# Attention values loaded in longer runs, into a third buffer, in another order

## The chip, the cores and the metric

One core of one Trainium2 chip runs the whole program. The metric is the device time of one execution in microseconds (us). A measurement of this kernel can tell about 0.2% (1.7 us) from no change.

## The reference

Three layers follow each other. The first is chunked local attention: each chunk of 32 queries sees 8 memory keys, 16 keys to the left, its own 32 and 8 to the right.

```python
def _attn_ref(q, k, v, mem_k, mem_v):          # B, H, S, D = 2, 8, 768, 64
    for c in range(S // 32):
        l_start, r_end = max(0, 32 * c - 16), min(S, 32 * c + 32 + 8)
        k_full = np.concatenate([mem_k, k[:, :, l_start:r_end]], axis=2)
        v_full = np.concatenate([mem_v, v[:, :, l_start:r_end]], axis=2)
        scores = scale * np.matmul(q[:, :, 32 * c:32 * c + 32], k_full.transpose(0, 1, 3, 2))
        a = np.exp(scores - np.max(scores, axis=-1, keepdims=True))
        a = a / (np.sum(a, axis=-1, keepdims=True) + 1e-09)
        out[:, :, 32 * c:32 * c + 32] = np.matmul(a, v_full)
...
def _moe_ref(x, domain_probs, w1, w2):         # 1536 tokens, 512 wide, 4 experts, 1024 inner
    p = domain_probs / (domain_probs.sum(-1, keepdims=True) + 1e-09)
    for e in range(E):
        out += p[:, e:e + 1] * (np.maximum(x @ w1[e], 0.0) @ w2[e])
...
def _moe2_ref(x, w_in, w_out, alpha):          # 2048 inner
    h = x @ w_in
    return (np.maximum(h, 0.0) + alpha * np.minimum(h, 0.0)) @ w_out
```

All data are float32.

## The kernel before

**Work.** Attention is cut into 24 half-units (`half_unit`). One is a block of 128 queries, that is four windows of 32, of four heads. The half-units of a block's eight heads follow each other, and so do those of the two batches. The two later layers run over the tokens in tiles, `gemm1` and `gemm2`, with each float32 number cut into a high and a low part, so that TensorE does three products for one.

**One half-unit.** TensorE makes the scores (32 small matmuls into `two`, which has one buffer). VectorE takes the row maximum `mx` and subtracts it into `pe_ring`; ScalarE makes the exponential in place. TensorE transposes (`t`), ScalarE copies that to `pt_ring`. TensorE multiplies with the values (16 matmuls into `x`); the values carry a column of ones, so that `x` also holds the sum of the weights. VectorE adds 1e-9 (`dn`), takes the reciprocal (`rd`) and scales into `xs_ring`. TensorE transposes once more (`xt`), and ScalarE copies that to `acc`, the input of the next layer. `prep_x` splits `acc` into `xh` and `xl`.

**Values.** A tile `v` has 128 rows, two heads of 64 keys each. For each pair of heads and each window a row holds 130 numbers: 65 for the upper head and 65 for the lower one, and of these two one half is zero, so that one matmul over 128 rows gives both heads. The zeros are written once, by memsets on GpSimd and VectorE, and the loads fill the rest. The array in memory has 520 numbers (2080 bytes) in a row for one half-unit; in the tile they are laid out in 8 pieces of 65 numbers (260 bytes) with a gap of 65 after each. There are `RINGV` buffers of values (2) and `RING` of queries and keys (4).

**Order.** Every engine runs its instructions in the order in which the program writes them; nothing is moved afterwards. The generators and their due times in `now` set that order while the program is written. `load_half(hu + RING)` stands behind the score matmuls of half-unit `hu`, and `load_v(hu + RINGV)` behind its `x` matmuls, both in SyncE's queue. Each DMA uses one of eight semaphores in turn, so that an issue can also have to wait for the DMA that used its semaphore before.

**Two stretches.** Up to 57.65 us, 16 cycles (`att_cycle`) do attention alone: a cycle takes the scores of half-unit `m`, the `xt` of `m-3`, the `x` of `m-2`, then `keep_warm` (4 or 5 matmuls on zeros, whose result nobody reads) and the `t` of `m-1`. From 57.65 to 91.7 us the other half-units are put between the matmuls of the first tile of the second layer (`att_poll`). After that TensorE has the two matrix layers alone.

Of the kernel before, what the change touches and what calls it, by code (L numbers as in the profile page):

```python
# [10 lines left out]
F32 = mybir.dt.float32  # L11
# [7 lines left out]
B, H, S, D = 2, 8, 768, 64  # L19
CH, LEFT, RIGHT, MEM = 32, 16, 8, 8  # L20
BLK = 128
WIN = CH
NW = BLK // WIN
# [8 lines left out]
P = 128  # L32
KD = DM // P
HH = H // 2
HP = HH // 2
QW, KW, VW = HP * BLK, HP * SPAN, HP * (D + 1)
# [29 lines left out]
def tile_kernel(ctx: ExitStack, tc: tile.TileContext, qk, v, wa, wq, dpt, alpha, out):  # L66
    nc = tc.nc
    scale = 1.0 / float(D) ** 0.5
    pe_, dve, act, pool, sync = (Pinned(tc, e) for e in (nc.tensor, nc.vector, nc.scalar, nc.gpsimd, nc.sync))
# [3 lines left out]
    bp = ctx.enter_context(tc.tile_pool(name="bp", bufs=1))  # L73
# [7 lines left out]
    def bank(name):  # L81
        taken[0] += 1
        if more and taken[0] % 4 == 0:
            return more[0].tile([P, 512], F32, tag="pm", name=name)
        return ps.tile([P, 512], F32, tag="ps", name=name)
# [67 lines left out]
    def prep_x(c0, n, fast):  # L153
        cs = slice(c0, c0 + n)
        b11, b12 = acc[:, 0:2, 0, cs], acc[:, 0:2, 1, cs]
        b21, b22 = acc[:, 2:4, 0, cs], acc[:, 2:4, 1, cs]

        st = bp.tile([P, 3, 2, n], F32, tag="fr" if change[0] and c0 // n % 2 else "st", name=f"st{c0}")
        e = dve if fast else pool
        sub = ALU.subtract  # L160
        act.copy(xh[:, 0:4, cs], acc[:, :, 0, cs])
        e.tensor_tensor(out=st[:, 0], in0=b12, in1=b11, op=sub)
        yield
        e.tensor_tensor(out=st[:, 1], in0=b22, in1=st[:, 0], op=sub)
        act.copy(xh[:, 4:6, cs], b22)
        yield
        e.tensor_tensor(out=st[:, 2], in0=b22, in1=b12, op=sub)
        pool.tensor_tensor(out=xl[:, 0:4, cs], in0=acc[:, :, 0, cs], in1=xh[:, 0:4, cs].bitcast(F32), op=sub)
        yield
        for z in (0, 1):  # L170
            r = slice(6 + 4 * z, 10 + 4 * z)
            t_ = st[:, z:z + 2].rearrange("p a b n -> p (a b) n")
            if z == 1:
                e.tensor_tensor(out=st[:, 1], in0=b21, in1=st[:, 1], op=sub)
                yield
            act.copy(xh[:, r, cs], t_)
            if z == 0:
                pool.tensor_tensor(out=xl[:, 4:6, cs], in0=b22, in1=xh[:, 4:6, cs].bitcast(F32), op=sub)
            yield
            e.tensor_tensor(out=xl[:, r, cs], in0=t_, in1=xh[:, r, cs].bitcast(F32), op=sub)  # L180
            yield
# [6 lines left out]
    def mm(*a, n, took=None, **kw):  # L188
        pe_.matmul(*a, **kw)
        now[0] += took or 0.013 + n / 2.4e3  # L190


    qk_t = [bp.tile([P, QW + KW], F32, tag="ggB", bufs=4, name=f"qk{i}") for i in range(RING)]
    v_t = [bp.tile([P, HP, NW, 2, D + 1], F32, tag="w2", bufs=4, name=f"v{i}") for i in range(RINGV)]
    for vt in v_t:
        for e in range(2):
            (pool, dve)[e].memset(vt[(1 - e) * D:(2 - e) * D, :, :, e], 0.0)
    pe_ring = bp.tile([P, 2, HP, 2, KEYS], F32, tag="ft", bufs=3, name="pe_ring")
    pt_ring = bp.tile([P, 2, HP, BLK], F32, tag="fr", name="pt_ring")
    xs_ring = bp.tile([P, 2, HP, 2, D], F32, tag="ft", bufs=3, name="xs_ring")  # L200

    def load_half(hu):
        if hu >= 2 * NU:
            return
        sync.dma_start(qk_t[hu % RING], qk[hu // 2, :, hu % 2])

    def load_v(hu):
        if hu >= 2 * NU:
            return
        for e in range(2):  # L210
            rows = slice(e * D, (e + 1) * D)
            sync.dma_start(v_t[hu % RINGV][rows, :, :, e].rearrange("p z w d -> p (z w) d"),
                           v[hu // 2, rows, hu % 2].rearrange("p (a d) -> p a d", d=D + 1))

    def half_unit(u, half):

        hu = 2 * u + half
        qv = qk_t[hu % RING][:, :QW].rearrange("p (z q) -> p z q", q=BLK)
        kv = qk_t[hu % RING][:, QW:].rearrange("p (z k) -> p z k", k=SPAN)
        vv = v_t[hu % RINGV].rearrange("p z w e d -> p z w (e d)")  # L220
        c, ab = divmod(u, 2)
        cols = slice(c * BLK, (c + 1) * BLK)
        hs = slice(2 * half, 2 * half + 2)
        nm = f"{u}_{half}"

        win = [slice(w * WIN, (w + 1) * WIN) for w in range(NW)]
        s_ps = two[:, :, :HP * KEYS].rearrange("p e (z k) -> p e z k", k=KEYS)
        now[0] += T_SW
        for z in range(HP):
            for w in range(NW):  # L230
                for e in range(2):
                    rows = slice(e * D, (e + 1) * D)
                    mm(s_ps[win[w], e, z], qv[rows, z, win[w]], kv[rows, z, w * STEP:w * STEP + KEYS], n=KEYS,
                       took=T_S, start=True, stop=True)
        load_half(hu + RING)
        mx = cp.tile([P, 2, HP], F32, tag="mx", bufs=4, name=f"mx{nm}")
        dve.tensor_reduce(out=mx, in_=s_ps, axis=AX.X, op=ALU.max)
        pe = pe_ring[:, hu % 2]
        dve.tensor_tensor(
            out=pe.rearrange("p z e k -> p e z k"), in0=s_ps,  # L240
            in1=mx.unsqueeze(3).to_broadcast([P, 2, HP, KEYS]), op=ALU.subtract,
        )
        yield LATE
        act.activation(pe, pe, AF.Exp, scale=scale)
        yield LAT[0]
        t_ps = bank(f"t{nm}")[:, :HP * BLK].rearrange("p (z q) -> p z q", q=BLK)
        now[0] += T_SW
        for z in range(HP):
            pe_.transpose(t_ps[:, z], pe[:, z].rearrange("p e k -> p (e k)"), ident)
            now[0] += T_T  # L250
        pt = pt_ring[:, hu % 2]
        act.copy(pt, t_ps)
        yield LAT[1]
        x_ps = bank(f"x{nm}")[:, :2 * VW].rearrange("p (z e d) -> p z e d", e=2, d=D + 1)
        now[0] += T_SW
        for z in range(HP):
            for w in range(NW):
                mm(x_ps[win[w], z].rearrange("p e d -> p (e d)"), pt[:, z, win[w]], vv[:, z, w], n=2 * (D + 1),
                   took=T_X, start=True, stop=True)
        load_v(hu + RINGV)  # L260
        dn = cp.tile([P, HP, 2, 1], F32, tag="dn", bufs=2, name=f"dn{nm}")
        dve.tensor_scalar_add(dn, x_ps[:, :, :, D:D + 1], 1e-9)
        rd = cp.tile([P, HP, 2, 1], F32, tag="rd", bufs=2, name=f"rd{nm}")
        dve.reciprocal(rd, dn)
        xs = xs_ring[:, hu % 2]
        dve.tensor_tensor(out=xs, in0=x_ps[:, :, :, :D], in1=rd.to_broadcast([P, HP, 2, D]), op=ALU.mult)
        yield LAT[2]
        xt_ps = bank(f"xt{nm}")[:, :2 * BLK].rearrange("p (c q) -> p c q", q=BLK)
        now[0] += T_SW
        for z in range(HP):  # L270
            pe_.transpose(xt_ps[:, z], xs[:, z].rearrange("p e d -> p (e d)"), ident)
            now[0] += T_T
        act.copy(acc[:, hs, ab, cols], xt_ps)
        if ab == 1 and half == 1:
            while att["x"] < c:
                yield 0.2
            for _ in prep_x(c * BLK, BLK, c in FAST):
                yield X_STEP[c]
            att["x"] = c + 1
# [47 lines left out]
    def att_cycle():  # L327
# [14 lines left out]
        def at(hu, stage):  # L342
            if hu in live and att["stage"][hu] == stage:
                advance(live[hu])

        x = live[m] = [now[0], half_unit(*divmod(m, 2)), m]
        att["live"].append(x)
        att["next"] += 1
# [15 lines left out]
    raws, w1, w2 = {}, {}, {}  # L364
# [68 lines left out]
    def weights():  # L433
        for p in range(NP):
            yield from prep_w(p)
# [49 lines left out]
    def stream(name, gen):  # L485
        streams[name] = [0.0, None, gen]
# [213 lines left out]
        order += [(1, k), (2, k - 1)]  # L700
    order += [(2, len(tiles) - 1)]

    for i in range(2):
        load_half(i)
        load_v(i)
    load_half(2)
    stream("w", weights())
    streams["w"][0] = PREP0
    acts = {}
# [7 lines left out]
    for i, (what, k) in enumerate(order):  # L717
        p, c0, n = tiles[k]
# [41 lines left out]
T_S, T_X, T_T, T_SW = 0.017, 0.06, 0.11, 0.1  # L760
# [11 lines left out]
T_CONV = 18.0  # L772
DT_X = 0.35
RING = 4
RINGV = 2
WARM = 18


# [72 lines left out]
```

## Time and profile before

| what | value |
|---|---|
| median of 3 runs | 858.92 us (858.74 to 859.26) |
| the profiled execution, its own time | 859.42 us |
| its span, first to last instruction | 857.6 us |
| TensorE busy | 827.4 us, 96% of the span |
| VectorE, ScalarE, GpSimd busy | 593.8, 337.7, 575.3 us |
| mean granted TensorE clock | 0.984 |
| queue of the loads and stores | 50752 packets, 70.75 MB |

The time of the execution is 1.8 us more than its span. Share of busy time is a mean over stages with different limits; the rows below separate them. Kilobytes of a transfer are of 1024 bytes, GB/s are of 10^9.

### The profile page before, as it was taken

To read this page: it belongs to the slowest core of one execution; us is meant where nothing else is said; L and a number is where in the kernel's file an instruction comes from. 1 tells how busy PE (TensorE), PEld (TensorE's weight loads), DVE (VectorE), ACT (ScalarE), POOL (GpSimd) and SP (SyncE) were. 2 spreads that over 40 slices of the span, in tenths; PEclk is the share of its full clock that TensorE was granted. 3 is DMA by queue.
4 is the path that set the end of the run, shared out by engine and by line. 5 is a ranking of instruction groups with operands and counts; after the bars stand their busy time and mean duration, and the time that the engine had idled before them with its cause. 6 is when DMAs were issued, how large, how long until landed. Compare 5 with 4: busy or idle time off the path is not lost.

```text
span 857.6 us, 15042 instructions
## 1 busy us (share of the span) xinstructions
PE 827.4 (96%) x5659; PEld 801.5 (93%) x5659; DVE 593.8 (69%) x1159; ACT 337.7 (39%) x754; POOL 575.3 (67%) x606
## 2 busy tenths in 40 slices
PE   7878999999999999999999999998899999999998
PEld 5655899999999999999999999997799999999998
DVE  3665847767677676777766786779777766776655
ACT  2544643223222231332332332325465645645442
POOL 2527566778659777678776777748576787764831
PEclk9998999999999999999999999999799999999999
DMA  9897202133213223213222212101012222111103
GB/s 217 185 214 174 63 24 73 56 100 105 87 38 102 89 80 100 87 38 120 89 80 82 86 63 88 72 1 50 25 50 74 75 87 98 63 62 38 62 1 148
DMA packets 50825, 71.71 MB, mean 84 GB/s; under 512 B 29120, under 2 KB 33344, under 8 KB 50752
## 3 DMA queue, kind: packets, MB, share of 16 engines
q1 hardware_dynamic: 50752, 70.75, 27.9%
q8 instruction: 44, 0.72, 0.4%
q14 instruction: 29, 0.24, 0.1%
HBM read 59.18 MB, written 11.56 MB: 82 GB/s over the span
## 4 chain that ended last, share of the span: by engine, by line
PE 85%; DMA 5%; DVE 4%; issue 2%; ACT 1%; SPq 1%; POOL 1%; POOLq 0%; DVEq 0%; ACTq 0%
PE y L60 45%; PE c L60 11%; PE a L60 11%; PE d L60 11%; PE b L60 5%; DMA v<-in_v 4%; DVE st L60 2%; PE x L60 1%; SPq L60 1%; DVE xl L60 1%; PE keep L60 1%; DMA qk<-in_qk 1%; ACT xh L60 1%; POOL gg L60 1%; DVE acc L60 1%
## 5 line engine op out<-in xcount | busy, mean ns | idle before, releaser
L60 PE MATMUL y<-gg,wh 128*128 128x384 f32 x1540 | 407.3, 341 | 7.1 <-POOL gg L60 4.4
L60 PEld LDWEIGHTS y<-gg,wh 128*128 128x128 f32 x1540 | 282.0, 190 | 11.0 <-POOL gg L60 6.8
L60 POOL TENSOR_TENSOR gg<-g,gg 128x384 fp32r<-128x384 f32 x192 | 199.6, 1049 | 109.2 <-ACT gg L60 98.9
L60 PE MATMUL y<-gg,wl 128*128 128x384 f32 (+1 forms) x770 | 260.6, 338 | 0.0
L60 DVE TENSOR_TENSOR acc<-y,acc 128x384 f32<-128x384 f32 x353 | 189.0, 551 | 68.3 <-PE y L60 66.8
L60 ACT CAST gg<-g 128x384 fp32r<-128x384 f32 x192 | 97.9, 512 | 163.7 <-DVE g L60 163.1
L60 POOL TENSOR_TENSOR wl<-raw,wh 128x256 fp32r<-128x256 f32 (+1 forms) x115 | 115.8, 1016 | 54.9 <-PE b L60 33.9
L60 PEld LDWEIGHTS y<-gg,wl 128*128 128x128 f32 x770 | 146.3, 190 | 0.0
L60 ACT COPY u<-a 128x384 f32<-128x384 f32 x48 | 23.1, 481 | 214.1 <-PE a L60 214.1
L60 POOL TENSOR_TENSOR wl<-s,wh 128x256 fp32r<-128x256 f32 x92 | 70.5, 773 | 10.5 <-ACT wh L60 10.3
L60 DVE TENSOR_TENSOR u<-b,u 128x384 f32<-128x384 f32 x48 | 26.7, 557 | 58.4 <-PE b L60 53.6
L60 PE MATMUL c<-xh,wh 128*128 128x384 f32 x192 | 64.7, 337 | 1.7 <-DVE b L60 1.7
L60 PE MATMUL c<-xh,wl 128*128 128x384 f32 x192 | 65.1, 339 | 0.0
L60 PE MATMUL d<-xh,wh 128*128 128x384 f32 x192 | 64.5, 336 | 0.4 <-DVE t L60 0.4
L60 PE MATMUL a<-xh,wh 128*128 128x384 f32 x192 | 64.7, 337 | 0.0
L60 PE MATMUL d<-xl,wh 128*128 128x384 f32 x192 | 64.1, 334 | 0.4 <-issue 0.4
L60 PE MATMUL a<-xl,wh 128*128 128x384 f32 x192 | 64.5, 336 | 0.0
L60 PE MATMUL c<-xl,wh 128*128 128x384 f32 x192 | 64.4, 335 | 0.0
L60 PE MATMUL a<-xh,wl 128*128 128x384 f32 x192 | 64.3, 335 | 0.0
L60 PE MATMUL d<-xh,wl 128*128 128x384 f32 x192 | 64.2, 334 | 0.0
L60 POOL TENSOR_TENSOR fl<-fl,fm 128x512 f32<-128x512 f32 x32 | 41.4, 1295 | 28.4 <-issue 16.8
L60 ACT CAST wh<-raw 128x256 fp32r<-128x256 f32 (+1 forms) x120 | 55.9, 489 | 0.6 <-PE a L60 0.6
(97 smaller groups left out, 1363.5 us busy)
## 6 DMA issues: line engine op xcount, KB each, us to landing
raw<-in_wa SPq DMA_DIRECT2D x32, 512.0 KB, 3.7
fr<-in_wq SPq DMA_DIRECT2D x32, 512.0 KB, 3.9
w2s<-fl SPq DMA_DIRECT2D x32, 256.0 KB, 2.3
raw<-w2s SPq DMA_DIRECT2D x16, 512.0 KB, 3.7
qk<-in_qk SPq DMA_DIRECT2D x24, 312.0 KB, 5.1
v<-in_v SPq DMA_DIRECT2D x48, 130.0 KB, 4.6
pb<-p_dram SPq DMA_DIRECT2D x8, 384.0 KB, 4.1
outT<-acc SPq DMA_DIRECT2D x15, 192.0 KB, 1.9
```

What stands on the lines that cost most here:

```text
L60: return self.tc.keep_in_program_order(f(*a, **kw))
```

## The change

Three things change. A value tile gets the head half as its outermost dimension inside a row, so that the 520 numbers of a load lie in one run of 2080 bytes and not in 8 of 260; an `x` matmul then reads its 130 numbers as two runs of 65, 2080 bytes apart. A third buffer of values is added; it consists of two tiles of one pair of heads each, whose loads are four of 1040-byte runs in place of two. Room for it comes from putting `pt_ring` and `xs_ring` in one tile, `late`. Last, the loads at the start are issued in another order.

```diff
-    v_t = [bp.tile([P, HP, NW, 2, D + 1], F32, tag="w2", bufs=4, name=f"v{i}") for i in range(RINGV)]
+    v_whole = [bp.tile([P, 2, HP, NW, D + 1], F32, tag="w2", bufs=4, name=f"v{i}") for i in range(2)]
+    v_t = [[t[:, :, z] for z in range(HP)] for t in v_whole]
+    v_t += [[bp.tile([P, 2, NW, D + 1], F32, tag="ft", bufs=3, name=f"v2_{z}") for z in range(HP)]]
     for vt in v_t:
-        for e in range(2):
-            (pool, dve)[e].memset(vt[(1 - e) * D:(2 - e) * D, :, :, e], 0.0)
+        for z in range(HP):
+            for e in range(2):
+                (pool, dve)[e].memset(vt[z][(1 - e) * D:(2 - e) * D, e], 0.0)
     pe_ring = bp.tile([P, 2, HP, 2, KEYS], F32, tag="ft", bufs=3, name="pe_ring")
-    pt_ring = bp.tile([P, 2, HP, BLK], F32, tag="fr", name="pt_ring")
-    xs_ring = bp.tile([P, 2, HP, 2, D], F32, tag="ft", bufs=3, name="xs_ring")
+    late = bp.tile([P, 4, HP * BLK], F32, tag="fr", name="late")
+    pt_ring = late[:, 0:2].rearrange("p r (z q) -> p r z q", q=BLK)
+    xs_ring = late[:, 2:4].rearrange("p r (z e d) -> p r z e d", e=2, d=D)
...
+        i = hu % RINGV
         for e in range(2):
             rows = slice(e * D, (e + 1) * D)
-            sync.dma_start(v_t[hu % RINGV][rows, :, :, e].rearrange("p z w d -> p (z w) d"),
-                           v[hu // 2, rows, hu % 2].rearrange("p (a d) -> p a d", d=D + 1))
+            src = v[hu // 2, rows, hu % 2]
+            if i < 2:
+                sync.dma_start(v_whole[i][rows, e].rearrange("p z w d -> p (z w d)"), src)
+            else:
+                for z in range(HP):
+                    sync.dma_start(v_t[i][z][rows, e].rearrange("p w d -> p (w d)"), src[:, z * VW // HP * NW:(z + 1) * VW // HP * NW])
...
-                mm(x_ps[win[w], z].rearrange("p e d -> p (e d)"), pt[:, z, win[w]], vv[:, z, w], n=2 * (D + 1),
-                   took=T_X, start=True, stop=True)
+                mm(x_ps[win[w], z], pt[:, z, win[w]], vv[z][:, :, w], n=2 * (D + 1), took=T_X, start=True, stop=True)
...
+    load_half(0)
     for i in range(2):
-        load_half(i)
+        load_half(i + 1)
         load_v(i)
-    load_half(2)
+    load_v(2)
...
-RINGV = 2
+RINGV = 3
```

On SyncE, at the start of the program, this is the difference; `qk_109` to `qk_112` are the four buffers of queries and keys, `v_113` and `v_114` the two whole buffers of values, `v_0_115` and `v_1_116` the two tiles of the third.

```order
 L60 DMA qk_109<-in_qk 128x624
-L60 DMA v_113<-in_v 64x8x65 x2
 L60 DMA qk_110<-in_qk 128x624
-L60 DMA v_114<-in_v 64x8x65 x2
+L60 DMA v_113<-in_v 64x520 x2
 L60 DMA qk_111<-in_qk 128x624
+L60 DMA v_114<-in_v 64x520 x2
+L60 DMA v_0_115<-in_v 64x260
+L60 DMA v_1_116<-in_v 64x260
+L60 DMA v_0_115<-in_v 64x260
+L60 DMA v_1_116<-in_v 64x260
 L60 DMA qk_109<-in_qk 128x624
```

The second and third loads of queries and keys move ahead of the values that stood before them, and four loads of the third buffer now stand ahead of the fourth and fifth loads of queries and keys.

The next rows are SyncE's queue of the changed program from the same place on, with the semaphores for which each issue waits; `DMAHW0` to `DMAHW7` are those of the DMAs, and a wait for one of them is a wait until an earlier DMA has landed. `raw_0_171` holds the first weights.

```order
L60 DMA v_0_115<-in_v 64x260
L60 DMA v_1_116<-in_v 64x260 [waits DMAHW0_49]
L60 DMA v_0_115<-in_v 64x260 [waits DMAHW1_49]
L60 DMA v_1_116<-in_v 64x260 [waits DMAHW2_49]
L60 DMA qk_109<-in_qk 128x624 [waits DMAHW3_49,PE_49]
L60 DMA qk_112<-in_qk 128x624 [waits DMAHW4_49]
L60 DMA raw_0_171<-in_wa 128x1024 [waits DMAHW5_49]
```

From the ninth DMA on every issue waits for the DMA eight places ahead of it. Before, the fourth and fifth loads of queries and keys were the eighth and ninth DMA of the program; now they are the eleventh and twelfth.

On TensorE, where the third half-unit's values are used for the first time:

```order
-L60 MATMUL xt_1_312<-ident,xs_ring 128x128 x2
-L60 MATMUL x_0_316<-v_113,pt_ring 32x130 x8
-L60 MATMUL keep_333<-xh 128x384 x4
-L60 MATMUL t_1_338<-ident,pe_ring 128x128 x2
+L60 MATMUL xt_1_325<-ident,late 128x128 x2
+L60 MATMUL x_0_329<-v_0_115,late 32x130 x4
+L60 MATMUL x_0_329<-v_1_116,late 32x130 x4
+L60 MATMUL keep_348<-xh 128x384 x4
+L60 MATMUL t_1_353<-ident,pe_ring 128x128 x2
```

Nothing changes its place on TensorE; the `x` matmuls of every third half-unit read two tiles in place of one.

## Rows read from the trace of the kernel before

**Rows 1.** The chain that ended last, its shares by line (page).

```profile
PE y L60 45%; PE c L60 11%; PE a L60 11%; PE d L60 11%; PE b L60 5%; DMA v<-in_v 4%; DVE st L60 2%; PE x L60 1%; SPq L60 1%; DVE xl L60 1%; PE keep L60 1%; DMA qk<-in_qk 1%; ACT xh L60 1%; POOL gg L60 1%; DVE acc L60 1%
```

**Rows 2.** Windows: length, busy time of each engine, TensorE's granted clock, DMA share, GB/s.

```profile
0.00:21.00 21.00, 15.78 (x262) 11.47 (x262) 7.49 (x23) 5.33 (x12) 5.88 (x13) 0.93 0.95 217
21.00:57.65 36.65, 28.91 (x615) 20.96 (x615) 22.22 (x68) 18.09 (x48) 15.58 (x17) 0.95 0.96 198
57.65:76.20 18.55, 13.91 (x293) 9.87 (x292) 11.06 (x34) 10.15 (x27) 11.24 (x12) 0.99 0.96 214
76.20:91.70 15.50, 15.19 (x222) 10.58 (x222) 12.10 (x30) 8.33 (x23) 9.92 (x11) 0.79 0.42 92
...
110.00:550.00 440.00, 440.00 (x2527) 439.93 (x2526) 312.61 (x586) 133.98 (x297) 324.70 (x342) 1.00 0.24 80
```

**Rows 3.** TensorE's waits up to 112 us: us in total, times, longest.

```profile
PE x L60 <- DMA v<-in_v: 10.9, 9, 2.8
PE two L60 <- DMA qk<-in_qk: 2.4, 2, 1.6
PE x L60 <- ACT acc L60: 1.2, 2, 0.9
...
PE x L60 <- ACT xh L60: 0.9, 2, 0.6
PE xt L60 <- DVE xs_ring L60: 0.8, 2, 0.6
```

**Rows 4.** Timeline of TensorE: start, length, operation, count [idle before, releaser].

```profile
44.55 0.98 PE L60 MATMUL keep<-xh 128*128 128x384 f32 x4
...
48.50 1.08 PE L60 MATMUL x<-v,pt_ring 128*32 128x130 f32 x16 [1.99 <-DMA v<-in_v]
49.50 1.65 PE L60 MATMUL keep<-xh 128*128 128x384 f32 x4
```

**Rows 5.** The chain in order of time: start, length, what.

```profile
21.91 0.58 PE x L60 x16
...
24.35 0.58 PE x L60 x16
...
44.67 0.60 SPq L60
...
45.33 7.73 DMA v<-in_v
...
53.15 0.65 PE x L60 x16
```

**Rows 6.** Tile view of the values: issue times (min/median/max ns), time to landing.

```profile
L60 SPq DMA_DIRECT2D v<-in_v x48: 595/596/1385, 1.2 to 85.7; - x48
...
DMA to landing us min/median/max: 3.2/4.6/7.7
```

**Rows 7.** The same view of the queries and keys.

```profile
L60 SPq DMA_DIRECT2D qk<-in_qk x24: 328/379/1655, 0.7 to 70.6; - x24
...
DMA to landing us min/median/max: 3.0/5.1/7.6
```

**Rows 8.** Packets of the whole span (page).

```profile
DMA packets 50825, 71.71 MB, mean 84 GB/s; under 512 B 29120, under 2 KB 33344, under 8 KB 50752
```

**Rows 9.** Two short windows, columns as in group 2.

```profile
10.00:12.00 2.00, 1.66 (x51) 1.36 (x52) 0.99 (x4) 0.14 (x1) 0.00 (x0) 1.00 1.03 417
...
16.00:18.00 2.00, 0.23 (x6) 0.07 (x5) 0.74 (x2) 0.79 (x2) 0.03 (x1) 0.96 1.22 202
```

**Rows 10.** Timeline of TensorE, the second group of score matmuls.

```profile
7.76 0.46 PE L60 MATMUL two<-qk 64*32 64x64 f32 x32 [1.63 <-DMA qk<-in_qk]
```

**Rows 11.** SyncE's queue waiting for earlier DMAs, first 100 us.

```profile
SPq L60 <- DMA v<-in_v: 3.3, 3, 1.9
```

**Rows 12.** The value tiles: the matmuls that read them, the memsets (ns).

```profile
L60 PE MATMUL x<-v,pt_ring x384: 271/274/428, 10.8 to 90.7; 128*32 128x130 f32 x192
...
L60 POOL MEMSET v<- x2: 532/532/532, 2.7 to 3.1; 64x520 f32 x2
```

More of the change, by code (lines that the diff above doesn't have):

```diff
@@ L219, in half_unit @@
         kv = qk_t[hu % RING][:, QW:].rearrange("p (z k) -> p z k", k=SPAN)
-        vv = v_t[hu % RINGV].rearrange("p z w e d -> p z w (e d)")
+        vv = v_t[hu % RINGV]
         c, ab = divmod(u, 2)
```

## The prediction

> **What bounds the kernel now.** The chain that ended last comes first: it shows which engine's work the end hangs on. Four fifths are TensorE's matrix products (`y`, `a`, `b`, `c`, `d`); the one other share above 2% is the wait for value loads, `DMA v<-in_v`, 4% or some 36 us [rows 1]. The windows say where. From 110 to 550 us TensorE is busy for 440.00 of 440 us at the full clock, so whatever is won before that moves everything after it forward one for one. Before 91.7 us TensorE idles: 5.2, 7.7, 4.6 and 0.3 us in the four stretches, and its granted clock is below 1, 0.79 in the last [rows 2]. TensorE's waits name the idle time up to 112 us: 10.9 us for values, 2.4 for queries and keys, and 2.9 for ScalarE and VectorE (1.2, 0.9 and 0.8) [rows 3].
>
> A wait costs a second time. [...] Windows price this: length times missing clock is 21.00 x 0.07, 36.65 x 0.05, 18.55 x 0.01 and 15.50 x 0.21; each times the busy share of its stretch (0.75, 0.79, 0.75, 0.98) makes 1.1 + 1.5 + 0.1 + 3.2 = 5.9 us [rows 2].
>
> Why values are late: with two buffers, the load for half-unit m+2 is issued after the `x` matmuls of m and must be there two cycles later. An undisturbed cycle goes from `x` at 21.91 to `x` at 24.35, 2.44 us. On the chain the load's first issue is at 44.67 us, the second load flies from 45.33 for 7.73 us, and the `x` for it starts at 53.15 [rows 5]. The median landing is 4.6 us, and two issues of 0.6 us stand ahead [rows 6], against 4.9 us for two cycles.
>
> **The change part by part.** *Runs of 2080 bytes.* Of the 29120 packets under 512 bytes, 48 x 64 x 8 = 24576 are value rows of 260 bytes [rows 6, 8]. How much DMA time these take: up to 91.7 us the DMA share times length is 20.0 + 35.2 + 17.8 + 6.5 = 79.5 us, and GB/s times length 17.2 MB. From 110 to 550 us, with long runs, a share of 0.24 moves 80 GB/s, 333 GB/s for a full share [rows 2]. Values are 48 x 133120 bytes = 6.4 MB; the other 10.8 MB at 333 GB/s take 32.5 us, so values take 47 us, at 136 GB/s. In a window of almost only values the queue moved 202 GB/s at a share of 1.22, and 417 GB/s at 1.03 where long runs were on their way [rows 9]; so 333 is no overstatement. In long runs the values take 6.4 / 0.333 = 19 us. The 79.5 us become 52 us. That is the queue's relief, not the program's: the program gets back what TensorE waited.
>
> *The third buffer.* The lead grows to three cycles, 7.3 us. Less about 1.4 us of issues, 5.9 us are left against a landing of 4.6 us in the median (7.7 at most) while the queue is full [rows 6]. With the queue relieved I take landings near the smallest of today, 3.2 us: both parts together should take away nearly all of the 10.9 us. Bounds: all 10.9, or half if the queue stays full. Its price: issues. A third half-unit has four loads in place of two. A load of queries and keys with 128 rows took 0.38 us to issue, a value load with 512 runs 0.6 [rows 6, 7]; with 64 runs I take 0.35 each, so 0.7 us for two and 1.4 for four, no more per cycle than the 1.2 us of today on average. Memsets: half as much again, 0.5 us more on GpSimd [rows 12], long before the first `x`, and VectorE's likewise; nothing.
>
> [...] A load of 130 KB lands in 4.6 us in the median, and one of 312 KB in 5.1 [rows 6, 7]: size hardly matters, and many loads overlap, since three landings, 14.3 us, fit in one cycle. [...] The four pieces are of 65 KB. If they ran one after the other at 3.2 us each, a set would take 12.8 us, 5.5 more than the lead, and eight sets would cost some 44 us; by the rows above they overlap, and cost nothing.
>
> *Order of the first loads.* The second scores waited 1.63 us [rows 10], and 2.4 us went to queries and keys in all [rows 3]. These loads now stand right behind the first, so I take 2.4 us as won. Against it, the fourth load of queries and keys is now the twelfth DMA and waits until the fifth has landed; it should land near 10.5 to 11 us, just when its cycle begins. Bounds: 2.4 us won, or 1 us lost again there.
>
> *`x` in two runs.* The tile's matmuls, 271 to 274 ns of which most is pipelined [rows 12], move on at 0.58 us for 16 [rows 5]. No row shows this read pattern; I take nothing, and as the other bound a doubling, 24 x 0.58 = 14 us. *`late`.* The same instructions wait for the same engines, so nothing.
>
> *What comes next.* Without the waits for values, ScalarE and VectorE have less time between `x` groups. VectorE is busy for 23.2 us of the 34.05 between 57.65 and 91.7 [rows 2], and that stretch shrinks to some 27. I let the 2.9 us that TensorE waits for these engines double. And the queue stays well filled: by 45 us it must bring 20 loads of queries and keys, 17 of values and 1.4 MB of weights and gates, 12.3 MB in 42 us, 293 GB/s of 333. I keep an eighth of the value waits, 1.3 us.
>
> **Sum.** Won: 10.9 + 2.4 + 5.9 = 19.2 us. Given back: 2.9 + 1.3 = 4.2. Net 15.0. The profiled execution took 859.42 us, 0.5 over the median of the runs; 858.92 - 15.0 = 843.9, so 844.
>
> **The rivals.**
> - *The queue stays the bound.* Queries and keys have long runs already and land no sooner than values [rows 6, 7], and 293 of 333 GB/s is close. Half of the value waits (5.5 us) and half of the lost clock (2.9) stay: 19.2 - 2.9 - 8.4 = 7.9 won, 851 us. Against it: 417 GB/s [rows 9].
> - *VectorE becomes the bound of the second stretch.* If it can be no busier than the 12.10 of 15.50 us of its last part [rows 2], its 23.2 us need 29.7 and not 27: 2.5 us less won, 846.5.
> - *Slower: eight DMAs in flight.* Every issue waits for the DMA eight places back. Three half-units take 11 DMAs where they took 9, so a landing time L forces 11/8 x L/3 = 0.46 L per half-unit. Today's mean is (91.7 - 4.6)/24 = 3.63 us, so it decides from a mean L of 7.9 us; at 8.5, 3.9 us each, 24 x 0.27 = 6.5 us, 865. For it: SyncE waited 3.3 us for earlier value loads already [rows 11]. Against it: today's longest landing is 7.7 [rows 6], and the packets get fewer.
> - *The four pieces serialize:* 844 + 44 = 888 us.
> - *`x` doubles:* 844 + 14 = 858 us, no change.
> - *The runs are not joined, and only the third buffer counts:* the loads still need their 79.5 us, and only the last stretch's and the first loads' waits go: some 5 us won, 854.
>
> **Chances.** Forecast 0.70 (its own range 839.5 to 848), queue 0.12, VectorE 0.09, eight in flight 0.03, serialized 0.02, `x` 0.02, not joined 0.02. The range reaches down to 838.5, where all 19.2 us and a little of the engines' waits are won, and up to 851.5 past the queue case. Faster by over 0.2% (1.7 us, about what a measurement of this kernel tells from no change): forecast, queue, VectorE and not joined, 0.93; within it 0.02; slower 0.05.
>
> **What would show it.** Right: TensorE's wait for values below 1.5 us and that for queries and keys near 0 up to 95 us; a granted clock of 0.99 or more up to there; some 20000 packets fewer under 512 bytes; landings of values near 3.2 us; the cycles of the first stretch near 2.5 us, its end near 46 us in place of 57.65; the long busy stretch of TensorE unchanged, only earlier. Wrong: a share of the DMA still near 0.95 up to the end of the first stretch, with landings above 4.5 us; `x` groups of more than 0.58 us at the full clock; SyncE waiting mainly for DMAs; waits for `acc`, `xs_ring` or `xh` of more than 6 us.

## The result and the profile after

The changed kernel takes 849.65 us (median of 6 runs, 846.88 to 852.80) and the kernel before 858.83 us (6 runs, 858.22 to 859.36). The ratio is 0.9895, 95% interval 0.9868 to 0.9923, so the time fell by 9.2 us, known to some 2.4 us to either side. The profiled execution took 848.56 us over a span of 846.8 us, at a mean granted clock of 0.988. The forecast was 844.0 with a range of 838.5 to 851.5: the direction and the range held, but 5.8 us of the 15 did not come, and the time lies above the 839.5 to 848 that the forecast gave as its own.

The first view is the page of the changed kernel: its packets and its chain.

```profile
DMA packets 30601, 71.71 MB, mean 85 GB/s; under 512 B 4800, under 2 KB 11072, under 8 KB 30528
...
PE y L60 45%; PE a L60 11%; PE c L60 11%; PE d L60 11%; PE b L60 5%; DVE st L60 2%; DMA v<-in_v 1%; PE keep L60 1%; PE x L60 1%; DVE xl L60 1%; PE two L60 1%; POOL gg L60 1%; POOL xl L60 1%; PE xt L60 1%; DVE acc L60 1%
```

The packets under 512 bytes fell from 29120 [rows 8] to 4800, by 24320, where the values had 24576; so the runs were joined. The share of value loads in the chain fell from 4% [rows 1] to 1%.

TensorE's waits up to 112 us after the change (total, times, longest), to be read against [rows 3]:

```profile
PE x L60 <- DMA v<-in_v: 2.5, 3, 1.6
PE xt L60 <- DVE late L60: 2.3, 3, 1.0
PE two L60 <- DMA qk<-in_qk: 2.1, 1, 2.1
...
PE x L60 <- ACT acc L60: 0.6, 1, 0.6
PE x L60 <- ACT late L60: 0.4, 1, 0.4
PE two L60 <- DVE pe_ring L60: 0.3, 1, 0.3
```

The waits for values went from 10.9 to 2.5 us. Those for queries and keys stayed, 2.4 before and 2.1 now, but all of it in one wait. Windows show the stages (columns as in [rows 2]; the first stretch now ends near 50, the whole attention near 81 us):

```profile
0.00:12.30 12.30, 9.05 (x149) 6.71 (x150) 4.98 (x17) 3.37 (x7) 3.62 (x13) 1.00 0.83 241
12.30:48.05 35.75, 32.10 (x706) 22.84 (x707) 25.07 (x77) 20.18 (x53) 18.07 (x21) 0.95 0.90 232
48.05:50.40 2.35, 2.35 (x20) 1.87 (x21) 1.79 (x6) 0.42 (x1) 0.52 (x1) 0.54 0.88 240
50.40:64.50 14.10, 13.97 (x289) 10.07 (x287) 9.27 (x29) 9.07 (x24) 9.28 (x11) 0.96 0.98 254
64.50:81.00 16.50, 13.75 (x228) 9.84 (x228) 14.74 (x36) 9.96 (x27) 12.69 (x13) 1.00 0.43 109
81.00:97.86 16.86, 16.11 (x91) 15.37 (x90) 13.15 (x23) 10.36 (x24) 7.30 (x8) 1.00 0.20 64
97.86:540.00 442.14, 442.14 (x2535) 442.09 (x2535) 312.48 (x587) 134.09 (x298) 326.28 (x343) 1.00 0.25 80
```

The share of the DMA engines is still 0.88 to 0.98 from 12.3 to 64.5 us: the queue was relieved far less than the forecast had it. From 97.86 us on TensorE is busy without a gap up to 540 us; the kernel before reached that, after the same work, at 109.52 us. The two rows up to that place, of before and then of after, are the account of the whole change:

```profile
0.00:109.52 109.52, 90.87 (x1480) 69.22 (x1480) 66.91 (x180) 53.19 (x135) 50.89 (x60) 0.94 0.76 167
```

```profile
0.00:97.86 97.86, 87.33 (x1479) 66.70 (x1480) 69.01 (x184) 53.36 (x135) 51.47 (x64) 0.97 0.70 187
```

TensorE is 11.66 us earlier. Its idle time fell from 109.52 - 90.87 = 18.65 to 97.86 - 87.33 = 10.53 us, 8.1 less, and the same matmuls were busy for 90.87 - 87.33 = 3.5 us less, at a mean granted clock of 0.97 where it had been 0.94. Behind this place 0.9 us are lost again (748.1 us from there to the end before, 748.9 after). The profiled executions add to the difference: that of before, 859.42 us, is 0.6 us above 858.83, and that of after 1.1 below its median. So 11.66 - 0.9 - 1.7 us make the 9.2 of the medians, up to rounding.

What is left of the waits is seen on TensorE's timeline (start, length, operation, idle before):

```profile
12.30 0.46 PE L60 MATMUL two<-qk 64*32 64x64 f32 x32 [2.09 <-DMA qk<-in_qk]
...
13.06 0.65 PE L60 MATMUL x<-v,late 128*32 128x130 f32 x16
13.64 1.28 PE L60 MATMUL keep<-xh 128*128 128x384 f32 x4
...
16.51 1.10 PE L60 MATMUL x<-v,late 128*32 128x130 f32 x16
...
48.05 0.98 PE L60 MATMUL x<-v,late 128*32 128x130 f32 x16 [1.63 <-DMA v<-in_v]
48.96 1.65 PE L60 MATMUL keep<-xh 128*128 128x384 f32 x4
```

The fourth scores stand still for 2.09 us, and the `x` of 16.51 us then takes 1.10 us, at a granted clock of 0.54 from 16.51 to 17.60 us, where the one of 13.06 took 0.65. The wait of 1.63 us at 48.05 is followed by a stretch with a granted clock of 0.54, and 0.50 from 48.30 to 50.40 us. So each of these waits is paid in part a second time: against 0.65 us for `x` and 0.98 for four `keep` [rows 4], the groups shown are 0.30 + 0.45 = 0.75 us longer behind the first wait and 0.33 + 0.67 = 1.00 behind the second. In the kernel before, TensorE waited most of the time from 16 to 18 us [rows 9], and the two microseconds behind that had this clock (columns as in [rows 2]):

```profile
18.00:20.00 2.00, 2.00 (x19) 1.61 (x20) 0.77 (x3) 0.00 (x0) 0.00 (x0) 0.50 0.85 178
```

SyncE's queue and the value tile after (issue times in ns; the timeline's columns are start, length of the issues, what):

```profile
17.23 2.38 SPq L60 DMA_DIRECT2D v<-in_v  x4
19.71 0.53 SPq L60 DMA_DIRECT2D qk<-in_qk  x1
20.34 1.10 SPq L60 DMA_DIRECT2D v<-in_v  x2
...
L60 SPq DMA_DIRECT2D v<-in_v x64: 465/568/1382, 1.7 to 69.7; - x64
DMA to landing us min/median/max: 2.5/5.0/7.0
...
L60 PE MATMUL x<-v,late x384: 271/273/428, 8.3 to 78.9; 128*32 128x130 f32 x192
```

A value load with 64 runs takes 0.57 us to issue in the median, hardly less than the 0.596 that it took with 512 [rows 6], though 0.465 at the least where that was 0.595. It lands after 5.0 us in the median where it was 4.6. The `x` matmuls that read two runs took 273 ns in the median, where they took 274 before [rows 12].

### The profile page after: what moved, and what is told of

Same layout as the page of the kernel before. It is cut to its first block, busy times and chain, and to the rows that moved or that the text cites. A ratio compares the mean times of both kernels' runs of the same rounds, so it can differ in the third digit from the quotient of the medians.

```text
span 846.8 us, 15093 instructions
## 1 busy us (share of the span) xinstructions
PE 824.5 (97%) x5659; PEld 799.8 (94%) x5659; DVE 593.6 (70%) x1163; ACT 337.6 (40%) x754; POOL 576.3 (68%) x610
## 4 chain that ended last, share of the span: by engine, by line
PE 88%; DVE 5%; DMA 2%; issue 2%; POOL 2%; ACT 1%; SPq 0%; DVEq 0%; POOLq 0%
PE y L60 45%; PE a L60 11%; PE c L60 11%; PE d L60 11%; PE b L60 5%; DVE st L60 2%; DMA v<-in_v 1%; PE keep L60 1%; PE x L60 1%; DVE xl L60 1%; PE two L60 1%; POOL gg L60 1%; POOL xl L60 1%; PE xt L60 1%; DVE acc L60 1%
```

## The experiments

Each kernel differs from the changed one by the edit shown; its ratio is to the kernel before, run beside it on the same chip. "GB/s at full share" is the last column divided by the DMA share in the window from 12.3 to 48 us, as a measure of how fast the queue goes while it is busy. For the changed kernel, from 12.30 to 48.00 us, that is 233 / 0.90 = 259.

The kernel before took 858.83 us beside the change, 860.42 beside two_buffers, short_runs, v2_later and interleaved, 859.32 beside old_order, qk3_early, interleaved_early and rows128_cut, and 859.40 beside the last three of the table: medians of different groups are compared by their ratios. Waits and GB/s are of one profiled execution each, which can lie at either end of the range: it was the slowest of its kernel for two_buffers, old_order, qk3_early and interleaved_whole, and the fastest for interleaved_early, rows128_cut and whole_early.

| kernel | median, us (range, runs) | ratio (95%) | TensorE waits: values / queries and keys / `xt` for VectorE, us | GB/s at full share |
|---|---|---|---|---|
| the change | 849.65 (846.88 to 852.80, 6) | 0.9895 (0.9868 to 0.9923) | 2.5 / 2.1 / 2.3 | 259 |
| two_buffers | 854.48 (852.25 to 855.64, 6) | 0.9922 (0.9895 to 0.9950) | 9.6 / 0 / 2.5 | 270 |
| short_runs | 856.66 (854.81 to 858.95, 9) | 0.9956 (0.9932 to 0.9980) | 6.7 / 2.7 / 0.7 | 215 |
| old_order | 851.41 (850.53 to 852.14, 4) | 0.9904 (0.9876 to 0.9932) | 3.8 / 1.4 / 2.9 | 252 |
| v2_later | 850.11 (848.11 to 851.43, 6) | 0.9870 (0.9842 to 0.9897) | 3.3 / 1.0 / 2.2 | 251 |
| qk3_early | 848.25 (847.66 to 851.69, 4) | 0.9876 (0.9845 to 0.9906) | 3.5 / 0 / 3.2 | 243 |
| interleaved | 849.09 (846.31 to 851.14, 6) | 0.9862 (0.9832 to 0.9891) | 0.4 / 3.1 / 3.2 | 307 |
| interleaved_early | 847.72 (845.36 to 850.44, 6) | 0.9871 (0.9844 to 0.9898) | 2.2 / 0.3 / 2.8 | 305 |
| rows128_cut | 844.54 (842.91 to 845.03, 4) | 0.9821 (0.9793 to 0.9849) | 0 / 0.5 / 2.6 | 299 |
| whole_early | 847.92 (846.42 to 850.34, 6) | 0.9864 (0.9836 to 0.9891) | 1.5 / 0 / 2.1 | 262 |
| two_queues_early | 852.89 (852.29 to 854.64, 6) | 0.9925 (0.9899 to 0.9951) | 0 / 0.4 / 1.1 | 252 |
| interleaved_whole | 844.93 (843.79 to 846.38, 6) | 0.9827 (0.9799 to 0.9854) | 0.7 / 0 / 4.5 | 307 |

Theory 1 is that a load into 64 rows that lie in one block of the tile is slow whatever the length of its runs. Theory 2 is that SyncE's time for issuing is what is left. Theory 3 is that the new place of the fourth load of queries and keys costs the missing time.

### The parts of the change, one undone at a time

**two_buffers** leaves out the third buffer:

```diff
-    v_t += [[bp.tile([P, 2, NW, D + 1], F32, tag="ft", bufs=3, name=f"v2_{z}") for z in range(HP)]]
...
-    load_v(2)
...
-RINGV = 3
+RINGV = 2
```

> The changed kernel with two buffers of values only (long runs and new order kept, no third buffer). The prediction's theory (long runs move values at 333 GB/s and bring landings to 3.2 us): a landing and two issues fit in two cycles of 4.9 us, so TensorE waits for values little more than with three buffers, about 850 us. The rival (a load of 64 rows side by side stays near 200 GB/s whatever its runs, so landings stay near 5 us): waits for values of 6 us or more come back, 853 to 856 us.

It took 854.48 us, in the range of the rival (853 to 856). Its waits for values are back:

```profile
PE x L60 <- DMA v<-in_v: 9.6, 6, 3.1
...
12.30:48.00 35.70, 26.70 (x599) 19.12 (x597) 21.64 (x66) 17.69 (x47) 15.61 (x19) 1.00 0.80 216
```

In this execution joined runs without the third buffer take away only 1.3 of the 10.9 us of value waits. With two buffers the share in the window is 0.80: the queue has pauses and the loads still come late. The clock of this window is 1.00 all the same, so not every wait brings a lower one. By its ratio two_buffers can't be told from the change (the intervals overlap).

**short_runs** has the three buffers and the order, with values in the old layout of 260-byte runs:

```diff
-    v_whole = [bp.tile([P, 2, HP, NW, D + 1], F32, tag="w2", bufs=4, name=f"v{i}") for i in range(2)]
+    v_whole = [bp.tile([P, HP, NW, 2, D + 1], F32, tag="w2", bufs=4, name=f"v{i}") for i in range(2)]
...
-                sync.dma_start(v_whole[i][rows, e].rearrange("p z w d -> p (z w d)"), src)
+                sync.dma_start(v_whole[i][rows, :, :, e].rearrange("p z w d -> p (z w) d"),
+                               src.rearrange("p (a d) -> p a d", d=D + 1))
...
```

> The changed kernel with the old layout of the values, runs of 260 bytes (three buffers and new order kept; the third buffer's loads are four of 260-byte runs). The queue has its old load of some 80 us at full share, so both theories expect it to stay the bound of the first stretch: the prediction said 854 us for it. If run length is what counts, its waits for values are several us above those of the changed kernel; if the third buffer alone does it, 850 us as with the change.

It took 856.66 us, and its interval lies above that of the change. The queue is full, and the value waits are 6.7 us:

```profile
PE x L60 <- DMA v<-in_v: 6.7, 6, 1.8
...
12.30:48.00 35.70, 30.59 (x649) 21.73 (x649) 21.32 (x68) 17.06 (x45) 15.37 (x18) 0.90 0.95 204
```

So both parts count, and neither alone gives the whole. The kernel beside them that has both, v2_later (the change but for the place of the third buffer's first loads), is 10.3 us below the kernel before; two_buffers is 5.9 below it and short_runs 3.8, and no execution of these two was as fast as the slowest of v2_later. As 5.9 and 3.8 make 9.7, the times don't show that the two parts need each other. The profiled executions look as if they did: the last `y` matmul that waits ahead of the long busy stretch starts at 108.89 us before and at 97.23 after the change, 11.7 earlier, but at 104.60 in two_buffers and 107.45 in short_runs, 4.3 and 1.4 earlier. That question stays open. The run length does count for the queue, but moderately: 215 GB/s at full share with short runs, 259 with long ones.

**old_order** puts the first loads back in the old order:

```diff
-    load_half(0)
     for i in range(2):
-        load_half(i + 1)
+        load_half(i)
         load_v(i)
+    load_half(2)
     load_v(2)
```

> The changed kernel with the first loads in the old order (each half-unit's values right behind its queries and keys), the third buffer's last. The second scores should wait again, by 1 us or more, and the fourth load stays the twelfth DMA. If the new order is worth the 2.4 us that the prediction gave it, 852 us; if what it wins is lost again at the fourth load in either order, 850 us.

It took 851.41 us, a ratio of 0.9904 (0.9876 to 0.9932), which can't be told from the change. The waits for queries and keys came to 1.4 us in three waits of at most 0.6 us, less than with the new order, and not the wait of 1 us or more at the second scores that was expected. This part of the change is not shown to bring anything.

### The fourth load of queries and keys

Two kernels move it relative to the third buffer's first loads: **v2_later** puts `load_v(2)` behind `load_half(3)`, one cycle into the program, and **qk3_early** puts `load_half(3)` ahead of `load_v(2)`.

```diff
-    load_v(2)
...
+        (1, lambda: load_v(2)),
```

> The changed kernel with the first loads of the third buffer behind the fourth and fifth loads of queries and keys. If the 2.1 us wait for queries and keys at 12.3 us and the low clock after it come from the place of these loads in the queue, both go: TensorE loses no time to queries and keys, 3 to 4 us less than the changed kernel, 846 us. If queries and keys are late for want of bandwidth, the wait stays and the time is that of the changed kernel.

```diff
+    load_half(3)
     load_v(2)
...
-        (1, lambda: load_half(3)),
```

> The changed kernel with only the fourth load of queries and keys moved ahead of the third buffer's first loads. If its place was why it came late: no wait for queries and keys, no low clock from 12 to 17 us, 3 us less than the changed kernel, 847 us. If bandwidth at the start was why: a wait of 1 us or more stays.

v2_later keeps 1.0 us of that wait and has a pause of 1.6 us in TensorE's own queue at scores; qk3_early removes the wait for queries and keys. But value waits were 3.3 and 3.5 us where the change had 2.5, and neither time, 850.11 and 848.25 us, can be told from that of the change; the 846 and 847 us expected did not come. Theory 3 names a true wait, 2.1 us; that removing it is worth time is not shown.

### The rows of a load

**interleaved** keeps the runs, the count and the size of every load, but puts the upper head's rows on the even rows of the tile and the lower head's on the odd ones, so that 64 rows are spread over all 128. The zeros are written over the whole tile first, and the first value loads wait for that.

```diff
...
-    pe_ring = bp.tile([P, 2, HP, 2, KEYS], F32, tag="ft", bufs=3, name="pe_ring")
+    pe_ring = bp.tile([P, 2, HP, KEYS, 2], F32, tag="ft", bufs=3, name="pe_ring")
...
-            rows = slice(e * D, (e + 1) * D)
-            src = v[hu // 2, rows, hu % 2]
+            rows = slice(e, P, 2)
+            src = v[hu // 2, e * D:(e + 1) * D, hu % 2]
...
```

> The changed kernel with the two heads' keys on every second partition in place of two blocks of 64, so that each load of 64 rows reaches over all 128 partitions; bytes, runs, number and order of loads as in the changed kernel. If blocks of 64 rows are what keeps the loads near 200 GB/s: DMA share from 12 to 48 us falls from 0.90 to about 0.7, landings of values from 5.0 to about 3.5 us, the waits for values (2.5 us) go, 846 to 847 us. If it is the ring of eight semaphores or the whole rate of the queue, nothing of this changes, 849 to 850 us. [...]

Its window from 12.3 to 48 us and its waits:

```profile
12.30:48.00 35.70, 32.61 (x722) 23.45 (x722) 25.03 (x75) 19.59 (x52) 17.45 (x20) 0.95 0.84 258
...
PE xt L60 <- DVE late L60: 3.2, 5, 1.0
PE two L60 <- DMA qk<-in_qk: 3.1, 1, 3.1
...
PE x L60 <- DMA v<-in_v: 0.4, 1, 0.4
```

The same loads at the same issue time (0.587 us in the median) now move 258 GB/s at a share of 0.84, 307 at full share where it was 259; values land in 4.3 us in the median in place of 5.0, queries and keys in 3.3 in place of 4.6, and the value waits are 0.4 us. So the rate bears out theory 1, by less than was expected (a share of about 0.7, landings of 3.5 us). It comes back with every such kernel: 299 to 307 GB/s at full share in the four whose value loads reach over all 128 rows, 243 to 270 in the seven with blocks of 64 rows and long runs. The time, 849.09 us, is not told apart from the change; 846 to 847 were expected. The first value loads now begin at 3.08 us, behind the zeros, where they began near 1.7, and the fourth queries and keys come 3.1 us late in place of 2.1.

**interleaved_early** mends that: the zeros are written buffer by buffer, and `load_half(3)` stands ahead of `load_v(2)` as in qk3_early.

> The changed kernel with the heads' keys on every second partition and the fourth load of queries and keys ahead of the third buffer's first loads, so that it is among the first eight DMAs. If the two remaining losses to DMAs are the slow loads of blocks of 64 rows and the fourth load's late place: TensorE waits less than 1 us for values and for queries and keys together, its clock stays at the full level up to 95 us, and 5 to 6 us go against the changed kernel: 844 us. If only one of the two is a cause, 847 us; if VectorE's waits take up what is won, 847 us too, with more than 6 us of waits for VectorE's tiles.

The wait for queries and keys is 0.3 us, but value waits are 2.2 us, at 305 GB/s for a full share. 847.72 us is not told apart from the change by the ratio; the 844 us that were expected if block and place are the two causes did not come.

**rows128_cut** loads the values over all 128 rows, two loads of half the run length (1040 bytes, 520 for the third buffer) in place of two of 64 rows. It leaves out part of the attention: the lower head's values land in the upper's columns and the second half stays zero.

```diff
...
-        for e in range(2):
-            rows = slice(e * D, (e + 1) * D)
-            src = v[hu // 2, rows, hu % 2]
+        src = v[hu // 2, :, hu % 2].rearrange("p (z g n) -> p z g n", z=HP, g=2)
+        for z in range(HP):
+            to = v_t[i][z][:, 0].rearrange("p (g a) d -> p g (a d)", g=2)
...
```

> The changed kernel with each load of values over all 128 rows, in half the run length (1040 bytes, and 520 for the third buffer), so that bytes and number of loads stay. It puts the lower head's values in the upper head's columns, so part of the attention is left out. If blocks of 64 rows are the cost: share and landings fall as with every second partition (307 GB/s for a full share, landings near 4.3 us or less), although the runs are shorter. If the run length is the cost: 250 GB/s for a full share or less, and more waits for values than with the change.

It took 844.54 us, ratio 0.9821 (0.9793 to 0.9849), which lies wholly below the interval of the change. Its window and its value tile:

```profile
12.30:48.00 35.70, 32.99 (x740) 23.60 (x730) 27.69 (x82) 21.70 (x58) 18.79 (x21) 1.00 0.87 260
...
L60 SPq DMA_DIRECT2D v<-in_v x64: 327/382/1477, 1.6 to 64.3; - x64
DMA to landing us min/median/max: 1.9/3.9/6.0
```

The same bytes in as many loads and in runs half as long, and there is no wait for values; the clock of the window is 1.00. The rate is that of interleaved; beside it a load takes 0.38 us to issue in place of 0.57. The kernel does not separate these two.

### The issues

**whole_early** is qk3_early with the third buffer in one tile, so that its loads are two and not four, 9 DMAs for three half-units in place of 11.

```diff
...
+    v_whole.append(bp.tile([P, 2, HP, NW, D + 1], F32, tag="fr", name="v2"))
...
-            if i < 2:
+            if i < 3:
...
```

> The changed kernel with the fourth load of queries and keys moved ahead and the third buffer in one piece, so that each half-unit's values are two loads; this swaps the places of the third buffer and of two small rings in memory. Nine DMAs for three half-units in place of eleven. New theory: SyncE issues almost without a break from 17 to 39 us, at 0.57 us for a load of 64 rows, so the number of issues is a bound by itself. Then the waits for values fall from 3.5 to about 1.5 us and the time to 846 us. If only the slow blocks of 64 rows count: waits for values near 3 us, 848 to 849 us.

```profile
PE x L60 <- DMA v<-in_v: 1.5, 2, 1.1
...
12.30:48.00 35.70, 31.41 (x679) 22.56 (x680) 26.63 (x81) 20.50 (x54) 18.65 (x21) 1.00 0.98 257
```

Value waits are 1.5 us where qk3_early had 3.5, as theory 2 expected, at the rate of blocks of 64 rows, 262 GB/s at full share, and a share of 0.98 where that was 0.93. But these are the slowest of qk3_early's executions (851.69 us) and the fastest of this kernel's (846.42). The time, 847.92 us, is not told apart from qk3_early's, and 846 were expected: that fewer issues shorten the program is not shown.

**two_queues_early** is qk3_early with the lower head's loads issued by ScalarE, which halves SyncE's work for values.

```diff
-                sync.dma_start(v_whole[i][rows, e].rearrange("p z w d -> p (z w d)"), src)
+                (sync, act)[e].dma_start(v_whole[i][rows, e].rearrange("p z w d -> p (z w d)"), src)
...
```

> The changed kernel with the fourth load of queries and keys moved ahead and the lower heads' value loads issued by ScalarE, so that SyncE issues about half as many; rows, runs, bytes and number of loads stay. If SyncE's issue time is a bound: waits for values below 1.5 us, unless ScalarE pays: its issues and waits then show as waits of TensorE for pt_ring, acc or pe_ring's exponential of several us more. If the blocks of 64 rows are the bound: waits for values stay near 3.5 us, 848 us or more.

It took 852.89 us, 0.9925 (0.9899 to 0.9951), above qk3_early's 0.9876 (0.9845 to 0.9906), though the intervals just overlap. TensorE's waits and the place of the longest, then VectorE and ScalarE at another:

```profile
PE x L60 <- ACT late L60: 7.5, 7, 3.0
PE t L60 <- ACT pe_ring L60: 2.2, 2, 1.4
...
20.41 0.65 PE L60 MATMUL x<-v,late 128*32 128x130 f32 x16 [2.96 <-ACT late L60]
...
25.67 0.42 DVE L60 TENSOR_TENSOR pe_ring<-two,mx 128x256 f32<-128x256 f32 x1
25.81 1.44 ACTq L60 DMA_DIRECT2D v<-in_v  x2
27.30 0.42 ACT L60 ACTIVATE pe_ring<-pe_ring 128x256 f32<-128x256 f32 x1 [1.32 <-PE t L60]
```

No `x` waits for values any more; 9.7 us of waits for ScalarE stand in their place. At 25.81 us two issues hold ScalarE's queue for 1.44 us. What the exponential behind them reads was ready at 25.67 + 0.42 = 26.09 us; it starts at 27.30, when the issues are done, 1.2 us late. ScalarE's own waits, by what ended them, show more of it:

```profile
ACT pe_ring L60 <- DMA qk<-in_qk: 3.3, 1, 3.3
...
ACT pe_ring L60 <- DMA raw<-in_wa: 2.1, 1, 2.1
...
ACT pe_ring L60 <- DMA v<-in_v: 1.8, 1, 1.8
```

The exponentials into `pe_ring` read none of these transfers. The issues ahead of them wait for earlier DMAs (one of eight semaphores each), and what stands behind an issue waits with it, as the exponential of 27.30 us did for 1.2 us: this is how the rows are read here, and no run takes one of these waits away by itself.

### Both together

**interleaved_whole** joins interleaved_early and whole_early: rows spread over 128, two loads for each half-unit, the fourth queries and keys early. It computes the whole reference.

> All that helped so far in one kernel that computes the whole reference: heads' keys on every second partition, the fourth load of queries and keys moved ahead, the third buffer in one piece. If the slow blocks and the number of issues are the two causes, no wait for values or queries above 0.5 us is left, the clock stays full, and the time is that of the loads over all 128 rows, 844.5 us. If a cause is missing, 846 to 848 us.

844.93 us (843.79 to 846.38), ratio 0.9827 (0.9799 to 0.9854). Its slowest run is below the fastest of the change, 846.88, and the intervals of the ratios don't touch. It is also the test of the rows in time: whole_early, measured beside it, has the same loads in blocks of 64 rows, and its fastest run, 846.42, is above the slowest here, 846.38. The medians are 3.0 us apart. The two profiles can't show where these 3.0 us lie, since they are of those two runs.

```profile
PE xt L60 <- DVE xs_ring L60: 4.5, 5, 1.5
...
PE x L60 <- DMA v<-in_v: 0.7, 1, 0.7
...
12.30:48.00 35.70, 31.66 (x697) 22.69 (x695) 25.89 (x80) 20.93 (x56) 18.59 (x21) 1.00 0.90 276
...
64.00:81.00 17.00, 14.52 (x179) 11.67 (x179) 15.11 (x32) 10.89 (x28) 13.51 (x13) 1.00 0.26 81
```

The queue moves 276 GB/s, the clock is 1.00, and the values are 0.7 us late in all. The largest wait left is for VectorE: 4.5 us for `xs_ring`. VectorE is busy for 15.11 of 17.00 us at the end of the attention, a share of 0.89; in the change it was the same, 14.74 of 16.50.

## Why the prediction was right, and where its size was off

**What held.** Value waits and the low clock that follows some of them (0.50 behind the one of 16 to 18 us before) were the gain: 10.9 us fell to 2.5, and TensorE's busy time for the same work by 3.5 us. Undoing either part gave some of it back: 4.4 us for the third buffer and 6.6 for the long runs, against v2_later. The packets joined as forecast, and the long busy stretch only moved.

**What did not.** The queue was not relieved as forecast, and most signs of it failed: value waits of 2.5 us and not below 1.5, 2.1 for queries and keys and not near 0, landings of 5.0 us and not 3.2, a clock of 0.97 and not 0.99, an end of the first stretch near 50 us and not 46. One of the signs of being wrong came, landings above 4.5 us. The range held since it was drawn to take in the rival "the queue stays the bound", to which the prediction gave a chance of 0.12.

**The terms.** Up to the place where TensorE is busy without a gap:

| term | forecast, us | measured, us |
|---|---|---|
| waits for values, less the eighth kept | 10.9 - 1.3 = 9.6 | 10.9 - 2.5 = 8.4 |
| waits for queries and keys | 2.4 | 2.4 - 2.1 = 0.3 |
| clock | 5.9 | 90.87 - 87.33 = 3.5 |
| waits for ScalarE and VectorE | -2.9 | 2.9 - 3.6 = -0.7 |
| sum | 15.0 | 11.5 (of 11.66 seen) |

**The step that failed** is "In long runs the values take 6.4 / 0.333 = 19 us." Share times length was 0.76 x 109.52 = 83.2 us before and is 0.70 x 97.86 = 68.5 now: 14.7 us fewer where 47 - 19 = 28 were forecast. So values take some 47 - 14.7 = 32 us, 6.4 MB / 32 us = 200 GB/s, an estimate from these rows. The 333 GB/s came from a stretch whose loads fill all 128 rows of a tile [rows 2], and it was taken over to loads of a block of 64 rows. interleaved shows that most of what is missing is the block. The first 97 us of the change and then of interleaved, which moves as many bytes there with nothing of a load changed but its rows:

```profile
0.00:97.00 97.00, 86.69 (x1476) 66.06 (x1476) 68.15 (x183) 52.98 (x134) 50.74 (x63) 0.96 0.71 189
...
0.00:97.00 97.00, 86.94 (x1483) 66.45 (x1484) 69.52 (x181) 53.73 (x135) 52.28 (x61) 0.98 0.62 189
```

The share falls by 0.09, that is 8.7 us of queue time out of the 32 - 19 = 13 that are missing, and the rate at full share rises from 259 to 307 GB/s. No run shows what the other 4 us are.

The value waits that are left hang on this in part: the share of the DMA stayed at 0.88 to 0.98 and landings at 5.0 us, not 3.2, as the rival "the queue stays the bound" had it. With spread rows the waits were 0.4, 2.2 and 0.7 us, so the rate alone does not settle them. The rival's 851 us is nearer to 849.65 than the forecast, though the lead of three cycles hid more than the half that it allowed. The runs that raise the rate and cut SyncE's time for issuing, rows128_cut and interleaved_whole, come out at 844.5 and 844.9, where the sum had put the change.

**The issue time** was a second mis-sized term: "with 64 runs I take 0.35 each" measured 0.57. No run shows what this costs the program by itself.

**The first loads** were the third: 2.4 us were taken as won. The wait moved from the second scores to the fourth, since that load "should land near 10.5 to 11 us" and landed at 12.2, as the chain after the change has it (start, length):

```profile
7.86 4.31 DMA qk<-in_qk
```

It is the thirteenth DMA of the program; the prediction and the section on the change count one too few. By SyncE's timeline the eight issues of values ahead of it took 1.19 + 3.66 = 4.85 us, 2 us more than 8 x 0.35. In rows128_cut, in the same order, they took 0.90 + 2.82 = 3.72 us, and TensorE waited 0.5 us for queries and keys and not 2.1: so the issue time is a likely part of this wait; the faster loads of that kernel can have helped, and no run parts the two. The bound of 1 us lost was too small. Given the kernels above, the new order is not shown to be better than the old.

**The rivals.** Serialized pieces are refuted by the page of the changed kernel, its DMA issues (count, KB each, median us to landing):

```profile
v<-in_v SPq DMA_DIRECT2D x32, 130.0 KB, 4.9
...
v<-in_v SPq DMA_DIRECT2D x32, 65.0 KB, 5.1
```

A piece of 65 KB lands 5.1 us after its issue and one of 130 KB 4.9, where four pieces one after the other would have taken 12.8. `x` in two runs cost nothing (273 ns for a matmul, 274 before). Eight in flight did not decide in the change, where SyncE waited for earlier DMAs for 1.4 + 1.2 + 0.5 = 3.1 us up to 52 us; in two_queues_early that was 8.7 + 6.9 + 1.6 = 17.2 us for the same three kinds of loads. VectorE as the next bound rested on a share of at most 0.78, and 14.74 of 16.50 us are 0.89; TensorE waited 2.6 us for it in the change (2.3 and 0.3). Whether it bounds interleaved_whole, with 4.5 us for `xs_ring`, no run tests.

**What stays open:** whether the lead and the longer runs need each other or only add up; how the gain of rows128_cut divides between rate and issue time; the 0.9 us lost behind the attention; and why six runs of the change spread over 5.9 us (those of before beside them over 1.1, but over 6.3 to 8.5 us in the later comparisons).

## What to carry to other kernels

Price a transfer from rows that have its own shape, its rows in the tile as well as its runs: joining runs helped here, but a block of 64 rows kept the queue at 259 GB/s for a full share where spread rows gave 307 (interleaved), and spreading the same rows over 128 gave another 3.0 us (whole_early to interleaved_whole). A buffer more and longer runs each brought a part of the gain alone (3.8 us in short_runs, 5.9 in two_buffers), and neither the whole. When one late load is moved ahead at the start, ask which load is now late in its place: here removing a wait of 2.1 us was not seen in the time, and values were waited for longer in the execution profiled.

## What the runs showed of the hardware

- A load of 64 rows took longer to issue than one of 128: 0.57 us in the median and 0.465 at the least for 64 rows in 64 runs (the change), 0.38 and 0.327 for 128 rows in 128 runs (rows128_cut). For 64 rows in 512 runs it was 0.596 and 0.595 (the kernel before). Why a load of fewer rows takes longer is not explained by any run.
- In the change a load of queries and keys took 0.33 us to issue by itself (at 16.06 us) and 0.53 right behind value loads of 64 rows (at 19.71 us).
- Loads of 64 rows spread over all 128 rows of a tile moved the queue at 305 to 307 GB/s for a full share, and loads of a block of 64 rows at 243 to 270 with runs as long and at 215 with runs of 260 bytes.
- In two_queues_early ScalarE issued a load in 0.49 us in the median, and TensorE waited 9.7 us for ScalarE.
